# Re-ordering one Strassen product: w_out sum ahead, quadrant sums in halves, products over changing banks

## The chip, the cores and the metric

The kernel runs on one NeuronCore of a Trainium2 chip. The metric is the device time of one execution in microseconds (us). Five runs of the kernel before gave 303.01, 303.22, 303.43, 304.36 and 303.58 us; the median is 303.43 us.

The core has engines that each work through an instruction list of their own, in order: PE (matrix products, with PEld loading the stationary operand), DVE (vector), ACT (scalar, exp), POOL (vector work, and issuing DMAs of the software queue) and SP (issuing DMAs of the hardware queue, among them DMA transposes). They wait for each other by semaphores.

## What is computed

Sparse attention followed by a two-layer network with a leaky activation. There are 8 batches, 8 heads, 576 positions, head size 64.

```python
scores = scale * np.matmul(q, k.transpose(0, 1, 3, 2))
# heads 0-3: a local band of 32; heads 4-7: keys with the same position mod 32, not later
scores = np.where(masks[None], scores, -1e9)
attn = softmax(scores)                       # (8, 8, 576, 576)
x = np.matmul(attn, v).transpose(0, 2, 1, 3).reshape(4608, 512)
h = x @ w_in                                 # (4608, 2048)
g = np.maximum(h, 0.0) + alpha * np.minimum(h, 0.0)
out = g @ w_out                              # (4608, 512)
```

## The kernel before, in words

**Chunks.** The 4608 tokens are worked in nine chunks of 512. A chunk's first layer ("lin1") makes the activation gT (2048 features on 16 blocks of 128 partitions, 512 tokens); its second layer ("lin2") multiplies gT with w_out. Chunk 0 is done plainly by `lin2_piece`. Chunks 1 to 8 use a Strassen-like product (`lin2_sums`): gT and w_out are cut into two by two quadrants, and seven products of quarter size, of which four use sums of quadrants of gT (gsum g1 to g4, made per chunk by `g_sum`, line 711) and some use sums of quadrants of w_out (wsum w1, w2, w4 and w3, the last made in place in w_out; made once by `w_sums`, line 699), give the four output quadrants o11, o12, o21, o22. g2 = g1 - quadrant, g4 = quadrant - g2, so g1, g2, g4 follow from one another; g3 needs gT alone. Also w1, w2, w4 follow from one another.

**Banks.** The seven products accumulate in three PSUM banks called A, B and C (tiles `hb`, which lin1 uses too). Product 0, 2, 4 and 6 go to A, one on top of the other; 1 and 3 go to B; 5 goes to C. After each product its bank's state is read out: products 0, 1, 2 and 6 are copied by ACT (line 771: o11, o22, o12, o21), products 3, 4 and 5 are added by DVE into a copy made before (line 774: o12, o22, o11) and the result is stored by SP. The next product on the same bank has to wait for that read-out. Each product is two halves of eight matmuls (128x128 by 256 columns), index `i` = 0 to 13, two for each product. For chunk 1 the order of the products is 0, 5, 1, 2, 3, 4, 6.

**Attention between.** Attention of the batches to come is cut into pieces (scores with exp on ACT and a mask on POOL; PV products; transposes of q and k; transposes of the result), which are put between the matmul groups of lin1 and lin2, so that PE always has work. How many go after each group is an accumulated count, `acc += left / divisor`; in the second half of chunk 1 (i >= 16 in the outer loop, line 977) the divisor is 21.7. Scores, PV results and transposes use the rotating PSUM pool `ps` with three buffers (`tp`, `tt`, `pv`, `sph`, `xp`), and `sp` with one. A PV result is read by DVE: reciprocal (line 478) and multiplication (line 480) into x, or x16s for the strided pairs.

**Where the attention result goes.** It must become xT, with features on partitions. From batch 2 on three of four head pairs are turned by DMA transposes issued by SP: the two local pairs straight into xT (line 506), the first strided pair from x16s into `xs` (line 504), which ACT then copies into xT in `x_copy` (line 511). The fourth pair is turned by PE in `x_piece` (tile `xp`, line 490) and copied into xT by ACT (line 191). Chunk 2's lin1 (line 629) needs all four pairs of batch 2: its matmuls go over kk = 0 to 3, one for each pair, so kk = 2 needs the copy of `xs` and kk = 3 the copy of `xp`. ACT has these in its list in the order: exp of a score, copy of `xs`, exp of the other half of the score, copy of o21 (line 771), copy of `xp`.

**Loads.** POOL issues loads of v (`vl`, `stv`), of q and k (`qsd`, `ksd`) and of their last rows (`tl`); SP issues `ql`, `kl`, the stores and the transposes. `load_v(3, False)` and `load_v(3, True)` stand in the chunk loop at fixed places of chunk 1 (lines 971 and 975).

**Order written out by hand.** Chunk 0's lin2 is a list of tokens (lines 939 to 952): ("M", i) is a quarter of a lin2 group, "S", "K", "P", "X", "T", "t" are attention pieces, "I" calls a function, here among others `w_sums`, which DVE carries out. w1 and w2 are made near the start of this list, w4 is made near its end, w3 at the start of chunk 1 (line 963).

Of the kernel before, what the change touches and what calls it, by code (L numbers as in the profile page):

```python
# [31 lines left out]
def kernel(  # L32
# [10 lines left out]
    nc = tc.nc  # L43
    keep = tc.keep_in_program_order

    B, H, S, D = q.shape
# [487 lines left out]
    for g in range(7, npair + 2):  # L534
        c = g // 4
        a, p, t = g, g - 1, g + 1
# [28 lines left out]
        for i, (kind, fn) in enumerate(seq):  # L565
            extra = []
            if todo and i in nslots:
                left = len([z for z in nslots if z >= i])
# [31 lines left out]
    def attn_until(b):  # L600

        return max(i for i, (g, _) in enumerate(pieces) if g == 4 * b + 3) + 1

    def attn_step(end):
        run_masks()
        if pos["i"] < end:
            pieces[pos["i"]][1]()
            pos["i"] += 1
        while late:
            late.pop(0)()  # L610
        if defer:
            defer.pop(0)()
# [26 lines left out]
    def lin1_piece(n, m):  # L639
        if n not in gTs:  # L640
            gTs[n] = gpool.tile([128, 16, 512], F16, tag="gT", name="gT")
        if n == 0 and m < 3:
            hps = lin1_mm(n, m, (0,), False, True)
        else:
            hps = lin1_mm(n, m, (3, 2, 0, 1) if n == 1 else range(4), True, True)

        neg = npool.tile([128, 512], F32, tag="neg", name="neg")
        keep(nc.scalar.activation(neg, hps, AF.Relu, scale=-1.0))  # L648

        def fin():  # L650
            keep(nc.vector.scalar_tensor_tensor(  # L651
                gTs[n][:, m, :], neg, oma[:, m : m + 1], hps, op0=ALU.mult, op1=ALU.add))
        late.append(fin)
# [25 lines left out]
    def quad(t, i, j):  # L679

        return t[:, 8 * j : 8 * j + 8, 256 * i : 256 * i + 256]

    def wq(i, j):

        return wout16[:, 8 * i : 8 * i + 8, 256 * j : 256 * j + 256]

    def w_sums(eng, which):

        w1, w2, w4 = wsum
        w3 = wq(0, 1)  # L690
        steps = {
            1: (w1, wq(0, 1), wq(0, 0), ALU.subtract),
            2: (w2, wq(1, 1), w1, ALU.subtract),
            3: (w3, wq(1, 1), wq(0, 1), ALU.subtract),
            4: (w4, wq(1, 0), w2, ALU.subtract),
        }
        for z in which:
            o, x, y, op = steps[z]
            keep(eng.tensor_tensor(o, x, y, op=op))

    def g_sum(eng, n, which, k0, k1):

        g = gTs[n]
        g1, g2, g4, g3 = gsum
        o, x, y, op = {
            1: (g1, quad(g, 1, 0), quad(g, 1, 1), ALU.add),
            2: (g2, g1, quad(g, 0, 0), ALU.subtract),
            3: (g3, quad(g, 0, 0), quad(g, 1, 0), ALU.subtract),
            4: (g4, quad(g, 0, 1), g2, ALU.subtract),
        }[which]  # L710
        keep(eng.tensor_tensor(o[:, k0:k1], x[:, k0:k1], y[:, k0:k1], op=op))  # L711
# [3 lines left out]
    def store(n, i, j, osb, mts=(0, 1)):  # L715

        r0 = 512 * n + 256 * i + 128 * mts[0]
        keep(nc.sync.dma_start(
            out[r0 : r0 + 128 * len(mts), 256 * j : 256 * j + 256].rearrange("(m p) c -> p m c", p=128),
            osb[:, mts[0] : mts[-1] + 1]))  # L720

    def quiet(n):

        return n >= NCH - 2

    def lin2_sums(n, i):

        g = gTs[n]
        last = n == NCH - 1
        p, mt = ((0, 5, 1, 2, 3, 4, 6) if n == 1 else range(7))[i // 2], i % 2  # L730
        if i == 0:
            tiles = [banks[z] for z in turn]
            lay.clear()
            for nm, t in zip("ABC", tiles):
                lay[nm] = [t[:, 0:256], t[:, 256:512]]
                lay[nm + "f"] = t
            turn[:] = [turn[1], turn[2], turn[0]]
            if last:
                lay["A"][1] = pspool.tile([128, 512], F32, tag="ps", name="opl")[:, 0:256]
            g_sum(nc.vector, n, 1, 4 if n == 1 else 6, 8)  # L740
            g_sum(nc.vector, n, 2, 0, 4)
            g_sum(nc.vector, n, 2, 4, 8)
        if i == (1 if quiet(n) else 2):
            g_sum(nc.vector, n, 4, 0, 8)
        if i == (2 if quiet(n) else 4):
            g_sum(nc.vector, n, 3, 0, 8)
        bank, lhs, rhs, first = (
            ("A", quad(g, 0, 0), wq(0, 0), True),
            ("B", gsum[0], wsum[0], True),
            ("A", gsum[1], wsum[1], False),  # L750
            ("B", gsum[2], wq(1, 1), False),
            ("A", gsum[3], wq(0, 1), False),
            ("C", quad(g, 0, 1), wq(1, 0), True),
            ("A", quad(g, 1, 1), wsum[2], False),
        )[p]
        dst = lay[bank][mt]
        own = mt == 0 or (last and bank == "A")
        for kf in range(8):
            keep(nc.tensor.matmul(  # L759
                dst, lhs[:, kf, 128 * mt : 128 * mt + 128], rhs[:, kf, :],  # L760
                start=(first and own and kf == 0), stop=(kf == 7), skip_group_check=True))

        def each(fn, o, *more):

            if last and bank == "A":
                fn(o[:, mt], lay["A"][mt], *[z[:, mt] for z in more])
            elif mt == 1:
                fn(o, lay[bank + "f"].rearrange("p (m c) -> p m c", m=2), *more)

        def act(o, x):  # L770
            keep(nc.scalar.copy(o, x))  # L771

        def add(o, x, y):
            keep(nc.vector.tensor_tensor(o, x, y, op=ALU.add))  # L774

        def new(nm):
            if mt == 0:
                held[nm] = opool.tile([128, 2, 256], F32, tag="osb", name=nm)
            return held[nm]

        if p == 0:
            each(act, new("o11"))
        elif p == 1:
            each(act, new("o22"))
        elif p == 2:
            each(act, new("o12"))
        elif p in (3, 4, 5):
            r, c = ((0, 1), (1, 1), (0, 0))[p - 3]
            o = held[f"o{r + 1}{c + 1}"]
            each(add, o, o)  # L790
            if mt:
                store(n, r, c, o)
        else:
            o21 = new("o21")
            if last and mt:
                keep(nc.vector.tensor_copy(o21[:, 1], lay["A"][1]))
            else:
                each(act, o21)
            if last:
                store(n, 1, 0, o21, (mt,))  # L800
            elif mt:
                store(n, 1, 0, o21)
# [113 lines left out]
    def attn_n(n, end):  # L916
        for _ in range(n):
            attn_step(end)
        if n == 0:
            attn_step(0)  # L920
# [7 lines left out]
    for z in (3, 4):  # L928
# [10 lines left out]
    run([  # L939
        ("M", 0), ("I", w_sums, nc.vector, (1,)), ("M", 4), ("I", w_sums, nc.vector, (2,)),  # L940
        ("I", load_qk, 2, False, "q"), ("M", 5), ("M", 1), ("M", 6), ("T", 3, "q"), ("M", 2),
        ("T", 3, "k"), ("t", 3), ("V", 1, 1, "dve"), ("C", 1, "q", 1, "dve"),
        ("C", 1, "q", 0, "pool"), ("V", 1, 0, "pool"), ("M", 7), ("C", 1, "k", 1, "pool"), ("M", 3),
        ("S", 6), ("T", 2, "q"), ("K", 6), ("M", 8), ("S", 7), ("t", 2),
        ("I", load_qk, 2, False, "k"), ("K", 7), ("M", 9), ("C", 1, "k", 0, "pool"), ("T", 2, "k"),
# [2 lines left out]
        ("I", load_d, 2), ("K", 4), ("M", 12), ("P", 6, 2), ("S", 5), ("O", 1, "pool", 1, 12),  # L948
        ("P", 4, 0), ("O", 1, "pool", 12, 24), ("X", 7), ("M", 13), ("I", cast_l, 2, "k", "act"),
        ("K", 5), ("P", 4, 1), ("I", load_v, 2, True), ("X", 6), ("M", 14), ("P", 5, 0), ("G",),  # L950
        ("P", 5, 1), ("M", 15), ("X", 4), ("X", 5), ("I", w_sums, nc.vector, (4,)), ("G",),
    ])
    assert pos["i"] == 2
    wide["on"] = False
# [3 lines left out]
    for n in range(1, NCH):  # L958
        ab = attn_until(n + 1) if n + 1 < B else len(pieces)
        left = ab - pos["i"]  # L960
        acc = 0.0
        if n == 1:
            w_sums(nc.vector, (3,))
        for i in range(30):
            second["on"] = i >= 16
            if i < 16:
                lin1_piece(n, {13: 7, 14: 14}.get(i, 8 * (i % 2) + i // 2))
                if i in (5, 9, 13) and (n, i) != (1, 13):
                    g_sum(nc.gpsimd, n, 1, i // 2 - 2, i // 2)
                if n == 1 and i == 14:  # L970
                    load_v(3, False)
            else:
                lin2_sums(n, i - 16)
                if n == 1 and i == 22:
                    load_v(3, True)
            if n < B - 2 or i < 16 or i > 19:
                acc += left / ((22.5 if i < 16 else 21.7) if n == 1 else 16 if n == B - 2 else 20.5) * (0.5 if i < 16 else 1.0)
            cnt = int(acc)
            acc -= cnt
            attn_n(cnt, ab)  # L980
        while pos["i"] < ab:
            attn_step(ab)
# [30 lines left out]
```

## Time and profile before

The profile is of one execution, whose own time and span stand beside the runs.

| what | value |
|---|---|
| median of five runs | 303.43 us |
| time of the profiled execution | 303.01 us |
| its span, first to last instruction | 301.2 us |
| granted TensorE clock | 0.998 |
| busy share PE / DVE / ACT / POOL | 97 / 76 / 60 / 55 % |
| chunk 1's lin2 on PE, first matmul of product 0 to the first of chunk 2's lin1 | 73.63 to 91.68 us |
| wholes of g4 and g3 in chunk 1 (DVE) | 2.18 and 1.21 us |
| w4 (DVE), at 57.52 us | 1.22 us |
| xs transpose of batch 2, issue | 84.07 us |

The profile has several views. The page gives busy time for each engine. The stages view gives the busy time of each engine in stretches of the span that one chooses. The timeline lists instructions in order of time: start in us, duration in us, engine, line, operation, output <- inputs, shapes, how many of them; in square brackets, how long the engine stood idle just before and what released it. The chain of waits follows the work that ended last back to the start. The DMA view gives for each issue the time from issue to landing. A matmul's recorded duration is a modelled end and longer than the distance to the next one; the starts are measured.

### The profile page before, as it was taken

What the parts mean: (1) busy time and instruction counts of PE and PEld (TensorE: products, weight loads), DVE (VectorE), ACT (ScalarE), POOL (GpSimd) and SP (SyncE); (2) the same over time, 40 slices, a digit from 0 to 9 for tenths busy, and PEclk for the clock granted to TensorE, in tenths of its full rate; (3) what the DMA queues carried; (4) which work ended last, traced back from release to release, by engine and by line L of the source; (5) the groups of instructions that cost most, each with busy time, mean ns of one, the idle gap of its engine ahead of it and who ended that gap; (6) DMA issues with size and microseconds to landing.
All of it is one profiled execution on the core that took longest, in us unless ns stands there. A gap on an engine that the chain in (4) does not pass through costs nothing.

```text
span 301.2 us, 7137 instructions
## 1 busy us (share of the span) xinstructions
PE 291.9 (97%) x2823; PEld 195.9 (65%) x2823; DVE 227.9 (76%) x429; ACT 180.5 (60%) x334; POOL 167.0 (55%) x176
## 2 busy tenths in 40 slices
PE   8899999999898999999999999999999999999995
PEld 3564456645774478647888887458745874784584
DVE  5788959989955987498848884888488958946872
ACT  3757458789537773776477746775577246506720
POOL 8952369379939965976497639772746003101300
PEclk9999999999999999999999999999999999999999
DMA  7999999997999996999499729971921040022004
GB/s 221 197 204 207 205 236 249 171 159 257 145 152 182 241 115 51 172 260 126 66 201 240 99 43 182 139 99 27 194 55 20 9 154 2 0 71 72 0 2 139
DMA packets 81713, 40.38 MB, mean 134 GB/s; under 512 B 58624, under 2 KB 77328, under 8 KB 81680
## 3 DMA queue, kind: packets, MB, share of 16 engines
q0 software_dynamic: 41728, 17.38, 52.0%
q1 hardware_dynamic: 39680, 22.03, 33.6%
q10 hardware_dynamic: 272, 0.52, 0.6%
q8 instruction: 22, 0.36, 0.5%
q14 instruction: 11, 0.09, 0.1%
HBM read 38.01 MB, written 9.44 MB: 158 GB/s over the span
## 4 chain that ended last, share of the span: by engine, by line
PE 77%; DMA 12%; DVE 5%; POOL 3%; ACT 1%; issue 1%; POOLq 0%
PE hb L629 35%; PE hb L759 30%; DMA qs<-in_q_dram 6%; PE pv L469 4%; DMA vl<-in_v_dram 3%; DMA tl<-in_k_dram 3%; PE hb L666 2%; DVE gsum L711 2%; PE sp L421 2%; PE tp L255 2%; PE opl L759 1%; DVE gT L651 1%; PE sph L421 1%; PE xp L490 1%; POOL vl L195 1%
## 5 line engine op out<-in xcount | busy, mean ns | idle before, releaser
L629 PE MATMUL hb<-xT,win 128*128 128x512 f16 (+1 forms) x616 | 127.8, 357 | 1.1 <-ACT xT L191 0.9
L651 DVE SCALAR_TENSOR_TENSOR gT<-neg,oma,hb 128x512 f16<-128x512 f32 x138 | 100.6, 744 | 33.1 <-ACT neg L648 26.6
L648 ACT ACTIVATE neg<-hb 128x512 f32<-128x512 f32 x138 | 82.0, 597 | 34.8 <-PE hb L629 34.1
L629 PEld LDWEIGHTS <-win 128*128 128x128 f16 x640 | 59.8, 98 | 54.6 <-issue 1.3
L711 POOL TENSOR_TENSOR gsum<-gT 128x512 f16<-128x512 f16 x23 | 26.4, 1148 | 52.0 <-DVE gT L651 52.0
L436 POOL TENSOR_TENSOR et<-et,consts 128x576 f16<-128x576 f16 (+1 forms) x24 | 31.2, 1300 | 42.4 <-ACT et L434 36.5
L759 PEld LDWEIGHTS <-gsum 128*128 128x128 f16 x512 | 47.4, 98 | 5.6 <-DVE gsum L711 0.2
L759 PEld LDWEIGHTS <-gT 128*128 128x128 f16 x384 | 35.9, 98 | 5.8 <-issue 0.4
L480 DVE TENSOR_TENSOR x<-pv,rc 96x384 f16<-96x384 f32 (+2 forms) x62 | 33.0, 532 | 2.1
L771 ACT COPY o<-hb 128x512 f32<-128x512 f32 (+1 forms) x32 | 18.1, 567 | 25.9 <-PE hb L759 25.9
L443 POOL TENSOR_TENSOR et<-et,consts 128x576 f16<-128x576 f16 (+1 forms) x24 | 31.4, 1310 | 2.1 <-ACT et L440 2.1
L759 PE MATMUL hb<-wout,gT 128*128 128x256 f16 x248 | 31.3, 273 | 0.0
L759 PE MATMUL hb<-wout,gsum 128*128 128x256 f16 x248 | 31.0, 273 | 0.0
L469 PEld LDWEIGHTS <-et 72*128 72x128 f16 (+1 forms) x448 | 23.7, 98 | 10.0 <-DVE x16s L480 1.1
L759 PE MATMUL hb<-wsum,gsum 128*128 128x256 f16 x248 | 30.1, 272 | 0.0
L774 DVE TENSOR_TENSOR o<-hb,o 128x512 f32<-128x512 f32 (+1 forms) x24 | 16.3, 680 | 14.9 <-PE hb L759 11.0
L434 ACT ACTIVATE et<-sp 128x576 f16<-128x576 f32 (+1 forms) x24 | 15.5, 645 | 18.6 <-PE sp L421 18.6
L478 DVE RECIPROCAL rc<-pv 72x6 f32<-72x6 f32 (+2 forms) x80 | 14.6, 182 | 8.7 <-PE pv L469 8.5
L440 ACT ACTIVATE et<-sph 128x288 f16<-128x288 f32 (+1 forms) x48 | 18.9, 409 | 0.0
L469 PE MATMUL pv<-vs,et 72*128 72x65 f16 x256 | 15.4, 194 | 0.9 <-DVE x16s L480 0.8
L195 POOL COPY vs<-stv 72x1024 f16<-72x1024 f16 x14 | 14.2, 1033 | 3.2 <-DMA stv<-in_v_dram 3.2
L759 PE MATMUL hb<-wsum,gT 128*128 128x256 f16 x120 | 15.2, 273 | 0.4 <-DVE o L774 0.4
(109 smaller groups left out, 326.2 us busy)
## 6 DMA issues: line engine op xcount, KB each, us to landing
out_dram<-o SPq DMA_DIRECT2D x31, 256.0 KB, 4.2
kl<-in_k_dram SPq DMA_DIRECT2D x6, 512.0 KB, 6.4
ql<-in_q_dram SPq DMA_DIRECT2D x5, 512.0 KB, 6.0
stv<-in_v_dram POOLq DMA_DIRECT2D x8, 288.0 KB, 7.6
vl<-in_v_dram POOLq DMA_DIRECT2D x6, 384.0 KB, 9.8
win<-in_moe_w_in_dram POOLq DMA_DIRECT2D x4, 512.0 KB, 11.2
wout<-in_moe_w_out_dram POOLq DMA_DIRECT2D x4, 512.0 KB, 15.9
qsd<-in_q_dram POOLq DMA_DIRECT2D x6, 288.0 KB, 7.0
```

What stands on the lines that cost most here:

```text
L195: keep(nc.gpsimd.tensor_copy(o, i))
L436: keep(nc.gpsimd.tensor_tensor(mv, mv, m, op=ALU.mult))
L440: keep(nc.scalar.activation(ev[:, n * y : n * y + n], sps[y][0:r, 0:n], AF.Exp, scale=SCALE))
L443: keep(nc.gpsimd.tensor_tensor(mv, mv, m, op=ALU.mult))
L469: keep(nc.tensor.matmul(pv[:, 65 * x : 65 * x + 65], et[0:r, c : c + 128], v16[0:r, 2 * P.pr + hh, t, :] if P.strided else v16[:, 6 * (2 * ...
L480: keep(nc.vector.tensor_tensor(P.x16[0:w, c0 : c0 + 64 * nb].rearrange("r (c e) -> r c e", e=64), pvv[:, :, 0:64], rc[0:w, 0:nb].unsqueeze ...
L629: keep(nc.tensor.matmul(hps[:, dst : dst + w], win16[:, kk, 128 * m : 128 * m + 128], xT[:, kk, src : src + w], start=(first and kk == kks ...
L648: keep(nc.scalar.activation(neg, hps, AF.Relu, scale=-1.0))
L651: keep(nc.vector.scalar_tensor_tensor(gTs[n][:, m, :], neg, oma[:, m : m + 1], hps, op0=ALU.mult, op1=ALU.add))
L711: keep(eng.tensor_tensor(o[:, k0:k1], x[:, k0:k1], y[:, k0:k1], op=op))
L759: keep(nc.tensor.matmul(dst, lhs[:, kf, 128 * mt : 128 * mt + 128], rhs[:, kf, :], start=(first and own and kf == 0), stop=(kf == 7), skip ...
L771: keep(nc.scalar.copy(o, x))
```

## The change

Four things are changed, all of them for chunk 1 alone. (1) The w4 sum moves from the end of chunk 0's token list to its beginning, behind w2. (2) g3 and g4 of chunk 1 are each made in two halves of four blocks, g3 at i = 4 and 5, g4 at i = 6 and 7; before, g4 was made whole at i = 2 and g3 whole at i = 4. (3) The products' order becomes 0, 5, 2, 1, 4, 3, 6, so that the banks go A C A B A B A where before they went A C B A B A A. (4) In the second half of chunk 1 the divisor becomes 19.7, so that attention pieces come more densely and end earlier, and `load_v(3, True)` is called two steps earlier.

```diff
-        p, mt = ((0, 5, 1, 2, 3, 4, 6) if n == 1 else range(7))[i // 2], i % 2
+        p, mt = ((0, 5, 2, 1, 4, 3, 6) if n == 1 else range(7))[i // 2], i % 2
...
-        if i == (1 if quiet(n) else 2):
+        if n == 1:
+            if 4 <= i < 8:
+                g_sum(nc.vector, n, 3 if i < 6 else 4, 4 * (i % 2), 4 * (i % 2) + 4)
+        elif i == (1 if quiet(n) else 2):
             g_sum(nc.vector, n, 4, 0, 8)
-        if i == (2 if quiet(n) else 4):
+        elif i == (2 if quiet(n) else 4):
             g_sum(nc.vector, n, 3, 0, 8)
...
         ("I", load_qk, 2, False, "q"), ("M", 5), ("M", 1), ("M", 6), ("T", 3, "q"), ("M", 2),
-        ("T", 3, "k"), ("t", 3), ("V", 1, 1, "dve"), ("C", 1, "q", 1, "dve"),
+        ("I", w_sums, nc.vector, (4,)), ("T", 3, "k"), ("t", 3), ("V", 1, 1, "dve"), ("C", 1, "q", 1, "dve"),
...
-        ("P", 5, 1), ("M", 15), ("X", 4), ("X", 5), ("I", w_sums, nc.vector, (4,)), ("G",),
+        ("P", 5, 1), ("M", 15), ("X", 4), ("X", 5), ("G",),
...
-                if n == 1 and i == 22:
+                if n == 1 and i == 20:
                     load_v(3, True)
...
-                acc += left / ((22.5 if i < 16 else 21.7) if n == 1 else 16 if n == B - 2 else 20.5) * (0.5 if i < 16 else 1.0)
+                acc += left / ((22.5 if i < 16 else 19.7) if n == 1 else 16 if n == B - 2 else 20.5) * (0.5 if i < 16 else 1.0)
```

What this does to the instruction lists of the engines: on PE the pieces of attention from the second product on stand one half product earlier, and the list is the same again from chunk 2's first matmul on. On DVE the read-outs of the first two PV results into x16s come before the sums g3 and g4. On ACT the copy of `xp` comes before the copy of o21. On POOL the load of `stv` comes before the two `tl` loads instead of behind them.

## The prediction

> **What bounds the kernel now.** I read the page first: PE is busy 97% of the span at a granted clock of 0.998, so time can be won only where PE stands still. The chain of waits runs on PE nearly all the way, except from 69.5 to 83 us, where it passes through ACT and DVE. So I cut the span into stages and looked where PE is not busy.
>
> ```profile
> 62.00:73.60 11.60, 11.60 (x99) 5.65 (x98) 9.62 (x17) 9.89 (x20) 10.70 (x10) 1.00 0.93 183
> 73.60:91.70 18.10, 16.53 (x224) 13.96 (x220) 14.05 (x28) 9.77 (x18) 13.29 (x13) 1.00 1.47 177
> 91.70:93.40 1.70, 0.82 (x9) 0.30 (x6) 0.00 (x0) 1.61 (x4) 1.68 (x3) 1.00 0.36 66
> ```
>
> The columns are stage, length, then PE, PEld, DVE, ACT and POOL busy. Stage two is chunk 1's Strassen product, the one that is edited; stage three is the start of chunk 2. PE is full before them. The timeline names each stop (idle time and releaser in brackets):
>
> ```profile
> 60.71 1.46 PE L629 MATMUL hb<-xT,win 128*128 128x512 f16 x6 [0.20 <-DVE gT L651]
> ...
> 77.72 2.18 DVE L711 TENSOR_TENSOR gsum<-gT,gsum 128x2048 f16<-128x2048 f16 x1
> 78.79 2.24 POOL L443 TENSOR_TENSOR et<-et,consts 72x576 f16<-72x576 f16 x1
> 80.66 0.62 PE L255 MATMUL tp<-consts,kl 128*128 128x128 f16 x8 [0.34 <-DVE x16s L480]
> 81.11 1.21 DVE L711 TENSOR_TENSOR gsum<-gT 128x2048 f16<-128x2048 f16 x1
> 83.08 0.30 PE L469 MATMUL pv<-vs,et 72*128 72x65 f16 x4 [0.81 <-DVE x16s L480]
> 84.07 1.21 SPq L504 DMA_TRANSPOSE xs<-x16s  x1
> 89.49 1.03 PE L759 MATMUL hb<-wsum,gT 128*128 128x256 f16 x8 [0.42 <-DVE o L774]
> 90.68 1.31 ACT L511 COPY xT<-xs 128x576 f16<-128x576 f16 x1 [0.69 <-DMA xs<-x16s]
> 91.90 0.40 ACT L440 ACTIVATE et<-sph 128x288 f16<-128x288 f32 x1
> 92.20 0.57 ACT L771 COPY o<-hb 128x512 f32<-128x512 f32 x1
> 92.67 0.65 ACT L191 COPY xT<-xp 128x576 f16<-128x576 f16 x1
> 93.37 0.81 PE L629 MATMUL hb<-xT,win 128*128 128x512 f16 x3 [0.88 <-ACT xT L191]
> ```
>
> Five stops, 2.65 us as shown. They cost more: eight 256-column matmuls pass in 0.87 us in the chain of waits, 0.109 each, while one is recorded as 0.272, so each stop hides 0.16 more. From start to start the stops lose 0.26 + 0.50 + 0.98 + 0.48 + 1.04 = 3.26 us (the first and fourth without the 0.10 that every score block costs on each side here). After 93.4 us the timeline shows PE starts without any such gap to the end, so what is won up to there should be kept.
>
> **Part 1, w4 moved.** Before, w4 takes DVE for 1.22 us at 57.52. ACT's tail copy of kT waits 0.35 for the tail copy of qT queued behind it, so the first `neg` starts at 59.06 and the first gT ends at 60.67, when PE needs it at 60.45. Without w4 ACT goes on at 58.55, `neg` ends about 59.33, gT about 60.08: the stop goes, **-0.26**. Next late is nothing: the second gT comes 0.75 later, PE asks 0.87 later. In its new place w4 follows w2 (ends 38.29) and DVE is idle for 2.30 us up to 40.60, so 1.22 fits: 0. POOL issues loads there; its two issues under w1 and w2 took 0.64 and 0.62, as alone (0.63), so again 0. At worst the vl load issued at 38.82 starts 0.7 later, and nobody needs it before 51.6.
>
> **Part 2, quadrant sums in halves and later.** Three PSUM tiles rotate through scores, transposes and PV. At 80.66 a transpose waits for DVE to read out a PV, queued behind g4 (2.18); at 83.08 a PV waits for the next read-out, queued behind g3 (1.21). In the new instruction order both read-outs come before the sums: x16s one ends near 78.25, two near 79.65, when PE asks for the tiles at 78.9 and 80.3. Both stops go, **-1.48**. Four halves at 0.68 (the row of the g2 halves) instead of two wholes at 1.21 are 0.30 us more of DVE, which then idles. By my walk g3 is whole near 81.5 and needed at 82.9, g4 near 83.4 and needed at 84.9; each slack is 1.4.
>
> [...]
>
> **Part 3, product order A C A B A B A.** The last product no longer meets bank A just after the product whose sum DVE still reads; that add (0.69) lies under the two B products, **-0.48**. The second A product, now right after C, needs g2 (ends about 77.4, asked for at 78.0) and bank A copied out (ACT, 76.19 to 76.78): 0. The next A product needs its o12 copied, near 81.5 against 82.9: 0.
>
> **Part 4, denser attention.** No instruction is added; from the second product on attention pieces move one half product (0.87) ahead. The first PV is then asked for at 75.57, while the tile it reuses is read out until 75.62 plus signalling: **+0.10**. Its masks are done (72.8 and 74.0). POOL is the serial engine here (10.70 of 11.60 us busy) and no mask moves ahead of its exp; with stv issued two steps earlier POOL's order becomes stv, tl, tl, and stv goes out near 80.1 instead of 82.28, with no one queued behind it but the tails, needed a chunk later. On ACT the xT copy of the last pair passes the o21 copy: 92.67 - 92.20 = 0.47 off the way to chunk 2. PE reaches chunk 2 at 91.68 - 0.26 - 1.96 + 0.10 = 89.56 and wants its fourth matmul (kk = 3) at 90.21.
>
> **Part 5, what is late next.** That matmul ran at 93.37. ACT was busy without a break from 90.68, when xs landed: copy, exp, o21, xT. With o21 out, kk = 3 can run at landing + 2.24 (93.37 - 0.47 - 90.66). Only a landing before 88.0 would give all of it. xs is issued when the third read-out ends: 82.1 against 84.07. When does it land? The DMA view, for the stretch 76 to 91 and for chunk 2:
>
> ```profile
> xs<-x16s SPq DMA_TRANSPOSE x1, 6.6
> ...
> xs<-x16s SPq DMA_TRANSPOSE x1, 4.4
> ```
>
> If it takes 6.6 again, it lands at 88.7, kk = 3 runs at 90.94 and the gain is 2.43. [...] The software queue holds vl, qsd, ksd, tl and stv from 74 on, and its last, stv, lands at 82.28 + 8.0 = 90.3; xs landed 0.4 after that, and the same transpose took 4.4 in chunk 2, where the software queue had nothing in that stretch. [...] The new xs has more of the crowded stretch ahead of it, but can use turns that its own queue may leave free between 82 and 85, when only one store and the end of one transpose stand before it; I take the middle, 89.7: kk = 3 at 91.92, **gain 93.37 - 91.92 = 1.45**.
>
> **Sum.** The profiled execution took 303.01 (span 301.2 and 1.8 around it); 303.01 - 1.45 = 301.56. Its time is the lowest of five, 0.42 under the median of 303.43, so the median becomes 301.98, predicted 302.0. The four stops inside (2.22) are won, and about 1.7 us comes back as a longer stop at the head of chunk 2.
>
> **The rivals.**
> - The drain rules (30%): xs lands at 90.3 to 90.7, gain 0.3 to 0.9, median about 302.9. For it: xs landed just behind stv. Against it: the stretch 82 to 85 has room in xs's own queue.
> - The transfer follows its issue or better (22%): landing 86.5 (82.1 + 4.4) to 88.7; gain 2.4 to 3.16, median near 300.6. For it: 4.4 in chunk 2. Against it: six loads are in flight.
> - Slower (6%): xs is overtaken. The o11 store (256 KB) goes out near 79 instead of 81.22 and stv 2 us sooner, both into the stretch in which pair 9's xT transpose took 10.0 us; if they push xs behind qT and kT's traffic, ACT, in order, holds xT, o21 and the first `neg` behind it. It decides from a landing after 91.1 (90.66 + 0.47) and passes the measurable from 92.0; at 93.3, where qT landed (85.38 + 7.9), the median would be 305.6. Against it: that same traffic was all ahead of xs before too.
> - My forecast (42%): landing 88.8 to 90.2, gain 0.9 to 2.3.
>
> That the change does not do what it says is out: the new order on each engine shows it.
>
> **Numbers.** A measurement of this kernel can tell about 0.3% (0.9 us) from no change. Faster by more: the forecast and the early landing, 0.64. Within: the drain, 0.30. Slower: 0.06. The range runs from nearly all stops won (303.43 - 3.16 = 300.3) to the drain with its smallest gain, 303.2.
>
> **What would show it.** Right: no PE idle on x16s between 76 and 83 nor on the o add before the last product; PE at chunk 2's first matmul near 89.5; xs issued near 82, landed near 89.7, ACT idle before the xs copy, and PE waiting about 1.7 us in two pieces (for the xs copy, then for xT). The drain: the same with landing beyond 90.2. Wrong: new idle on g3 or g4, a PV that waits for a POOL mask, w4 delaying the gT of chunk 0 or a first-pass read-out, or new gaps after chunk 2 has begun.

## The result and the profile after

The changed kernel takes 303.11 us (median of 43 runs, 300.71 to 309.74) against 303.64 for the kernel before (80 runs in the same comparison): a ratio of 0.9975, with a 95% interval of 0.9961 to 0.9989, or by that ratio 0.76 us less (0.53 between the medians). The ratio leaves out runs more than 1.5% above the fastest of their kernel. I had predicted 302.0, a gain of 1.45. The sign is right; the size is about half.

The profiled execution took 301.8 us, 1.2 less than the one of before, and it does nearly what the prediction said. The stages first (stage, length, then PE, PEld, DVE, ACT and POOL busy, the granted clock, DMA share, GB/s):

```profile
62.00:74.00 12.00, 12.00 (x99) 5.82 (x98) 9.84 (x18) 10.29 (x22) 11.85 (x11) 1.00 0.70 171
74.00:90.32 16.32, 16.30 (x223) 13.98 (x221) 13.17 (x30) 8.93 (x18) 12.55 (x12) 1.00 1.39 187
90.32:92.17 1.85, 0.98 (x6) 0.29 (x4) 0.00 (x0) 1.85 (x4) 1.83 (x3) 1.00 1.47 90
```

The product now lasts 16.3 us and PE is busy in all of it; before, the same work took 18.1 with 16.5 busy. What is left is the third row, the head of chunk 2. The timeline, at the places where before stood still:

```profile
61.13 1.90 PE L629 MATMUL hb<-xT,win 128*128 128x512 f16 x8
...
79.90 0.61 PE L255 MATMUL tp<-consts,kl 128*128 128x128 f16 x8
...
81.33 0.29 PE L469 MATMUL pv<-vs,et 72*128 72x65 f16 x4
...
82.38 1.25 SPq L504 DMA_TRANSPOSE xs<-x16s  x1
...
88.31 1.04 PE L762 MATMUL hb<-wsum,gT 128*128 128x256 f16 x8
...
89.97 1.31 ACT L511 COPY xT<-xs 128x576 f16<-128x576 f16 x1 [1.74 <-DMA xs<-x16s]
91.33 0.38 PE L629 MATMUL hb<-xT,win 128*128 128x512 f16 x1 [0.42 <-ACT xT L511]
91.49 0.63 ACT L191 COPY xT<-xp 128x576 f16<-128x576 f16 x1
92.17 2.10 PE L629 MATMUL hb<-xT,win 128*128 128x512 f16 x9 [0.46 <-ACT xT L191]
```

Four PE rows that carried a bracket before have none. ACT, which stood idle for 0.69 us before the copy of xs, now does so for 1.74, and PE waits at two places, for that copy and for the copy of xT behind it. From start to start these two stops lose 0.58 and 0.62 us. The DMA view has the landing of xs, 7.6 us after its issue where before had 6.6:

```profile
xs<-x16s SPq DMA_TRANSPOSE x1, 7.6
```

From chunk 1's first matmul to the fourth of chunk 2 this execution needs 34.08 us (58.09 to 92.17) where before needed 35.97 (57.40 to 93.37): 1.89 less. But chunk 1 began 0.69 later, and 1.89 - 0.69 = 1.20 is the difference of the two executions. The 0.69 comes from chunk 0, which the prediction had put at 0. The first two rows are of before, in the timeline:

```profile
50.30 2.29 POOL L195 COPY vl<-vl 32x715 f16<-32x715 f16 x2
51.08 0.81 DVE L329 TENSOR_TENSOR et<-et,consts 128x576 f16<-128x576 f16 x2
```

and these of after:

```profile
50.48 1.78 POOL L195 COPY vl<-vl 32x715 f16<-32x715 f16 x2
50.87 1.71 DVE L329 TENSOR_TENSOR et<-et,consts 128x576 f16<-128x576 f16 x2
51.63 0.36 PE L469 MATMUL pv<-vl,et 128*128 128x65 f16 x6 [0.25 <-DVE et L329]
53.18 0.36 PE L469 MATMUL pv<-vl,et 128*128 128x65 f16 x6
53.87 0.43 PE L490 MATMUL xp<-consts,x 72*128 72x72 f16 x8 [0.33 <-DVE x L480]
```

The same two POOL copies and the same two DVE masks meet, and now the masks take longer and the copies less: before, the copies take 2.29 and the masks 0.81; after, 1.78 and 1.71. PE, which was 0.21 us ahead of before until then, pays for the second order with stops of 0.42, 0.24 and 0.50 us, where before lost 0.16 and 0.10.

A last thing is seen in the times and not in this execution. Each run has a mean granted clock. Of the 44 runs of the changed kernel (the profiled one too) 29 have 0.998 or more, with a median of 302.27. The other 15 have 0.986 to 0.994 and take 303.8 to 309.7, with a median of 306.15. Without those, the gain would be 303.64 - 302.27 = 1.37, nearly the forecast (the clocks of the 80 runs of before are not listed in this comparison). This is what the experiments pursue.

### The profile page after: what moved, and what is told of

It is laid out like the page before. It is cut to its first block, busy times and chain, and to the rows that moved or that the text cites. A ratio compares the mean times of both kernels' runs of the same rounds, so it can differ in the third digit from the quotient of the medians.

```text
span 300.0 us, 7141 instructions
## 1 busy us (share of the span) xinstructions
PE 291.5 (97%) x2823; PEld 195.4 (65%) x2823; DVE 228.2 (76%) x431; ACT 180.1 (60%) x334; POOL 166.4 (55%) x176
## 3 DMA queue, kind: packets, MB, share of 16 engines
q1 hardware_dynamic: 39680, 22.03, 32.7%
## 4 chain that ended last, share of the span: by engine, by line
PE 77%; DMA 14%; DVE 3%; POOL 3%; issue 1%; ACT 0%; ACTq 0%; DVEq 0%; POOLq 0%
PE hb L629 37%; PE hb L762 29%; DMA qs<-in_q_dram 6%; PE pv L469 3%; DMA vl<-in_v_dram 3%; DMA xs<-x16s 3%; DMA tl<-in_k_dram 2%; PE tp L255 2%; PE sp L421 2%; PE opl L762 1%; PE hb L666 1%; DVE x L480 1%; PE sph L421 1%; PE xp L490 1%; DVE et L329 1%
## 5 line engine op out<-in xcount | busy, mean ns | idle before, releaser
L648 ACT ACTIVATE neg<-hb 128x512 f32<-128x512 f32 x138 | 82.1, 597 | 34.6 <-PE hb L629 33.9
L436 POOL TENSOR_TENSOR et<-et,consts 128x576 f16<-128x576 f16 (+1 forms) x24 | 31.9, 1328 | 42.4 <-ACT et L434 35.5
L711 POOL TENSOR_TENSOR gsum<-gT 128x512 f16<-128x512 f16 x23 | 26.4, 1148 | 52.0 <-DVE gT L651 52.0
L777 DVE TENSOR_TENSOR o<-hb,o 128x512 f32<-128x512 f32 (+1 forms) x24 | 16.3, 681 | 16.1 <-PE hb L762 12.4
L666 PE MATMUL hb<-wout,gT 128*128 128x512 f16 x64 | 15.6, 379 | 0.0
## 6 DMA issues: line engine op xcount, KB each, us to landing
wout<-in_moe_w_out_dram POOLq DMA_DIRECT2D x4, 512.0 KB, 16.3
```

The lines of the kernel that those rows point to most:

```text
L436: keep(nc.gpsimd.tensor_tensor(mv, mv, m, op=ALU.mult))
L666: keep(nc.tensor.matmul(ops, gTs[n][:, kf, 128 * mt : 128 * mt + 128], wout16[:, kf, :], start=(kf == 0), stop=(kf == 15)))
```

## The experiments

Four theories. **G**: PE's stops are now gathered at the head of chunk 2, and there the clock falls to half in some runs. **C**: xs lands when the transfers in flight have drained, however early it is issued (the prediction's rival). **W**: w4 in its new place brings the stops of chunk 0. **T**, formed later: xs lands late where the transpose of pair 9 meets the vl load. The recorded expectations use more letters: A is the first form of G (a lower clock in some runs), B is W; N (the stops of chunk 0 come and go, whatever is done to w4) and S (the early store and stv load, or the chip, delay xs) are rivals. "Low-clock runs" are those with a mean clock under 0.995; no run has a value between 0.994 and 0.997. Their share is given as "5 of 22".

### The parts, apart

**e1, the changed kernel again**, with no edit.

> The changed kernel again, beside the kernel before on the same chip. Theory A (granted clock): at a full granted clock of 1.00 the changed kernel is 1.4 us faster than before, and the measured 0.76 is what is left because some of its runs get a clock near 0.993, which costs 0.7% of some 290 us of PE, 2 us; so runs sorted by their clock fall into groups 2 us or more apart, and those at 1.00 lie near 302.2. Theory B (w4): every run is 0.7 us late at the start of chunk 1, as in the profiled one (chunk 1's first matmul at 58.09 instead of 57.40), so the gain is 0.7 at any clock. Theory C (landing): the time varies with the landing of xs; this profile shows a stop at the head of chunk 2 other than 1.2 us.

302.48 us (10 runs), ratio 0.996 [0.9938, 0.9983]; 1 of 10 low-clock (before on this chip 0 of 23). In its profile xs lands 8.0 us after its issue and the two stops at the head of chunk 2 are 1.04 and 0.62; the stops of chunk 0 are there again.

**e2, only w4 moved.**

```diff
+        ("I", w_sums, nc.vector, (4,)), ("T", 3, "k"), ("t", 3), ("V", 1, 1, "dve"), ("C", 1, "q", 1, "dve"),
...
-        ("P", 5, 1), ("M", 15), ("X", 4), ("X", 5), ("I", w_sums, nc.vector, (4,)), ("G",),
+        ("P", 5, 1), ("M", 15), ("X", 4), ("X", 5), ("G",),
```

> Only the w4 sum is moved; sums, product order and attention as before. Theory B: it is the loss: chunk 1 begins near 58.1 and the time is 0.4 to 0.7 us above before. Theory A, and the prediction: -0.26 at the head of chunk 1, which the later wait for xs takes back, so between 0 and -0.26, not measurable; chunk 1 begins near 57.4, give or take what the run to run difference of the first stage is.

303.59 us, ratio 1.0001 [0.9986, 1.0016], no low-clock run in 13. The gT stop at the head of chunk 1 is gone (from the first matmul of chunk 1 to the product 15.97 us instead of 16.23, as predicted), and the stops of chunk 0 have come (0.41, 0.23, 0.50). As a whole it gains nothing.

**e3, all but w4**: the edit of e2 undone in the changed kernel.

> The changed kernel with w4 made where it was before. Theory B: faster than the whole change by 0.4 to 0.7 us, so 1.2 to 1.5 us below before. Theory A: like the whole change within 0.3 us, since w4 gives only 0.26 which the wait for xs takes back. Theory C: the same as A.

302.14 us, ratio 0.9954 [0.9942, 0.9967], 1 of 6 low-clock. No stops of 0.4 to 0.5 in chunk 0; the product takes 16.26 us; stops of 0.80 and 0.62 at the head of chunk 2. So the three other parts give all of the gain that can be measured; of these only the sums were tried by themselves (e7).

**e7, only the sums in halves and later.** In the old order of products g4 is asked for first, so it is made first here.

```diff
+        if n == 1:
+            if 4 <= i < 8:
+                g_sum(nc.vector, n, 4 if i < 6 else 3, 4 * (i % 2), 4 * (i % 2) + 4)
```

> Only the quadrant sums in halves and later, on the kernel before; the fourth before the third, since the old order of products asks for it first. By the prediction's steps both stops inside (0.50 and 0.98) go and xs is issued near 82.4 instead of 84.07. If the landing binds (theory C), it lands near 90, the xT copy of the last pair still waits for o21, and the fourth matmul of chunk 2 runs at landing + 2.7 = 92.6: a gain of 0.7, near 302.8, with the stop of 0.48 before the last product kept and simply filled into the wait. If the parts add up (rival), the gain is 1.48, near 302.0.

302.36 us (22 runs), ratio 0.9982 [0.996, 1.0004], 5 of 22 low-clock; the other 17 have a median of 302.11. Both inner stops are gone, the one before the last product stays (0.48 as the prediction counts it). xs, issued at 83.50, lands at 90.82, and kk = 3 runs at 93.53, which is landing + 2.71, as theory C has it, for o21 is still ahead of the xT copy. From chunk 1's first matmul that is 35.20 us, 0.77 less than before. The two do not agree: the trace has C's gain, near 0.7, but the 17 runs lie 1.48 under before, which is just what the rival said. One profile is one landing.

### Does an earlier issue bring an earlier landing?

The profiles of the kernels that keep pair 10's DMA transpose answer it. Counted from the first matmul of chunk 1 (issue, landing): before 26.7, 33.3; e2 26.4, 31.2; e12 (below) 26.4, 31.0; e7 25.2, 32.5; e3 24.6, 32.3; the changed kernel 24.3, 31.9; e1 24.3, 32.3; e16 (below) 24.3, 32.7. The three that issue xs latest have it at 31.0 to 33.3, the four that issue it earliest at 31.9 to 32.7: issued two microseconds sooner, xs does not land sooner. The DMA view of e2, where xs was issued latest:

```profile
xs<-x16s SPq DMA_TRANSPOSE x1, 4.8
```

4.8 us there, 7.6 in the changed kernel. These landings agree with theory C. I had taken the middle between this and a landing that follows the issue; that it came near (89.95 for 89.7) is in part luck, for the reason I gave, room left in xs's own queue, is not what these profiles show.

One thing holds in all fifteen profiles with this transpose: xs lands within 0.7 us of the last of the loads that POOL issues at that time (stv and the two tl), whether these end at 88.7 us (e13, xs at 88.9) or at 93.7 (e9, below, xs at 93.6). For the changed kernel, and for e5 (below):

```profile
tl<-in_k_dram POOLq DMA_DIRECT2D x1, 32.0 KB, 8.2
...
tl<-in_k_dram POOLq DMA_DIRECT2D x1, 32.0 KB, 12.4
```

Issued at 81.81 and 80.78 us, they land at 90.0 and 93.2; xs lands at 90.0 and 92.9. In the five profiles without the transpose these loads end at 89.3 to 93.4, so they can end late without it.

### Is it the stop that costs the clock?

**e8, the stop made longer**: ACT copies the transposed pair 10 twice.

```diff
-        keep(nc.scalar.copy(
...
+        for _ in range(2 if P.g == 10 else 1):
+            keep(nc.scalar.copy(
```

> The changed kernel, with ACT's copy of the transposed pair 10 done twice over, so that PE's stop at the head of chunk 2 is 1.3 us longer (2.5 to 3.0 in all within some 4 us). Theory G (a concentrated stop lets PE's clock fall to half for one 3.4 us unit, in some runs): the runs with a mean clock under 0.995 become the rule, and the median is 1.3 + 1.7 to 2.0 over that of the changed kernel, near 305.5; the profile shows a piece of half clock after 92. Rival (the low clock in some runs has nothing to do with this stop): nearly all runs stay at 0.998 or more and the median is 303.7.

305.49 us (17 runs), ratio 1.0049 [1.0026, 1.0073]. The six runs at full clock have 303.71, as both theories had it; 11 of 17 are low-clock, ten of them at 0.992 to 0.994 with a median of 305.95. In the profile the two stops are 1.88 and 0.62 us, and the stages (the column before the last two is the clock) show what follows:

```profile
91.60:93.90 2.30, 0.61 (x4) 0.21 (x3) 0.00 (x0) 2.27 (x3) 2.28 (x3) 1.00 1.23 119
...
95.20:98.60 3.40, 3.40 (x15) 1.33 (x14) 1.49 (x2) 1.21 (x4) 3.40 (x4) 0.52 1.08 281
98.60:102.00 3.40, 3.40 (x35) 1.57 (x32) 2.71 (x5) 2.66 (x6) 0.69 (x2) 1.00 1.24 326
```

For one stretch of 3.4 us the clock is about half: 0.52, with 0.94 in the 1.3 us ahead of it and 1.00 behind. The nine matmuls from the end of the second stop on take 3.76 us, where the same nine took 2.10 in the changed kernel's profile (its row at 92.17): 1.7 us lost. (The counts of matmuls in the two stretches, 15 and 35, mix long and short ones.) In this run the half clock came after stops of 1.88 and 0.62; why some runs have it and others do not is not shown. Theory G holds as far as this: with the longer stop more runs lose their clock, 11 of 17 for 20 of 68.

**e5, w4 left out.** It is not computed at all, and the last product takes w2.

```diff
-            ("A", quad(g, 1, 1), wsum[2], False),
+            ("A", quad(g, 1, 1), wsum[1], False),
...
-        ("I", w_sums, nc.vector, (4,)), ("T", 3, "k"), ("t", 3), ("V", 1, 1, "dve"), ("C", 1, "q", 1, "dve"),
+        ("T", 3, "k"), ("t", 3), ("V", 1, 1, "dve"), ("C", 1, "q", 1, "dve"),
```

> The changed kernel without the w4 sum: it is not computed at all, and the last product takes w2 in its place, so its output is not the reference's. Theory W (w4 in its new place turns the order in which DVE masks and POOL copies get their turn in chunk 0, and that costs the stops of 0.4, 0.2 and 0.5 us there): the stops at 51 to 56 us are absent, the gT stop at the head of chunk 1 is absent too, and the median is 1.6 us under before, near 301.8. Rival N (those stops come and go with the landing of kl, whatever is done to w4): they can be there, chunk 1 begins as late as in the changed kernel, and the median is that of the changed kernel, near 302.4.

303.87 us (22 runs), ratio 0.9986 [0.9967, 1.0006]; 7 of 22 low-clock (before on this chip 2 of 58), the other 15 with a median of 302.50. The profile happened on a low-clock run (0.988) and shows one such run. Its DMA view, timeline and stages:

```profile
xs<-x16s SPq DMA_TRANSPOSE x1, 11.5
```

```profile
89.29 0.59 PE L629 MATMUL hb<-xT,win 128*128 128x512 f16 x2
92.89 1.31 ACT L511 COPY xT<-xs 128x576 f16<-128x576 f16 x1 [5.69 <-DMA xs<-x16s]
94.25 0.58 PE L629 MATMUL hb<-xT,win 128*128 128x512 f16 x1 [4.36 <-ACT xT L511]
```

```profile
89.29:92.80 3.51, 0.59 (x4) 0.19 (x2) 0.00 (x0) 0.00 (x0) 1.87 (x2) 1.00 1.56 78
92.80:96.20 3.40, 1.70 (x4) 0.51 (x4) 0.00 (x0) 3.13 (x5) 3.38 (x5) 0.51 1.11 197
96.20:99.60 3.40, 3.40 (x14) 1.39 (x13) 1.49 (x2) 1.12 (x3) 3.40 (x4) 0.50 1.07 238
```

xs lands 11.5 us after its issue instead of 7.6. PE, which reached chunk 2 at 89.29, over a microsecond sooner than in the changed kernel's profile, stands still for 4.5 us and then has half clock for 6.8 us, in some 5 of which it works. So in this run the late landing comes first, and the clock is the second payment for it.

**e9, PE kept busy in the stop**: seven matmuls of a zero tile, added into the same bank.

```diff
+            if n == 2 and m == 0 and kk >= 2:
+                for _ in range({2: 4, 3: 3}[kk]):
+                    keep(nc.tensor.matmul(
+                        hps, zer, win16[:, 0, 0:512], start=False, stop=False, skip_group_check=True))
```

> The changed kernel with seven 512-column matmuls of a zero tile at the head of chunk 2 (four before the fourth-last wait, for pair 10's xT, three before the wait for pair 11's), added into the same PSUM bank, so that PE works through 1.5 us of the 1.2 to 1.7 us in which it would stand still; the waits themselves stay. Theory G (the clock falls to half in some runs because PE stands still there): no run, or hardly any, under a mean clock of 0.995, where the changed kernel had 15 of 44; the median is that of its undisturbed runs plus at most 0.3, near 302.4. Rival (low-clock runs have another cause, for instance the chip): the low-clock runs stay about a third.

303.25 us (22 runs), ratio 0.9978 [0.9956, 1.0], and still 7 of 22 low-clock: the expectation failed. The profile, again of a low-clock run (0.987), shows a reason: xs landed 12.1 us after its issue, and PE stood still for 4.26 us behind the first six matmuls (two of chunk 2, four of zeros). 1.5 us of work cannot cover that.

**e4, pair 10 turned by PE** in the changed kernel, so that nothing at the head of chunk 2 waits for a DMA transpose.

```diff
-        P.xd = P.b >= DX and P.hp < 3
+        P.xd = P.b >= DX and P.hp < 3 and g != 10
```

> The changed kernel, with the first strided pair of batch 2 turned by PE (8 more matmuls of 72 columns, about 0.25 us) and not by a DMA transpose, so that chunk 2 no longer waits for a landing. All theories: the two stops at the head of chunk 2 (0.58 and 0.62 in the profile after) go, and with the 0.25 us for the matmuls the time is 0.9 us below the whole change. Theory C, that the landing mostly comes later than in the profiled run: more than 1.2 us below it, and less spread from run to run. If the next thing that is late (the copy of the last pair on ACT) takes their place: no more than 0.3 us.

302.21 us (5 runs), ratio 0.9961 [0.9948, 0.9974], none low-clock. The stop at the head of chunk 2 is gone. In the profile a new one has come (0.90 and 0.25 near 81): the additional piece shifts the attention, and two halves of g2 that meet two POOL masks (1.29 and 1.74) take 3.47 us instead of 1.28. The median is only 0.27 under e1's on the same chip, the case in which something else takes the stop's place.

**e6, the same with w4 in its old place**, and with the attention of chunk 1's first half kept where it was (one piece taken off the count `left` while i < 16).

> All of the change but the w4 move, and pair 10 turned by PE instead of by the DMA transpose; the attention of the first half of chunk 1 keeps its places. Theory: the wait at the head of chunk 2 is for the transposed pair alone, and the four stops inside were really won. Then PE stops only for the gT (0.36) and the first PV (0.2) and does 8 transposes more (0.26): 3.26 - 0.36 - 0.10 - 0.26 = 2.5 us under before, near 300.9, with every run at a mean clock of 0.998 or more, since PE nowhere waits longer than 0.4. Rival: DVE's second g2 half meets a POOL mask again as with pair 10 on PE before (3.47 for two halves, 0.90 + 0.25 of stop): near 302.0.

301.88 us (10 runs), ratio 0.9944 [0.9925, 0.9964], none low-clock. The new stop is gone, the product takes 16.25 us, and at the head PE waits only for pair 11's copy, 0.47 from start to start. The profiled execution took 301.17, near the forecast of 300.9; the median missed it by 1 us. The rows:

```profile
90.38 0.81 PE L629 MATMUL hb<-xT,win 128*128 128x512 f16 x3
91.49 2.10 PE L629 MATMUL hb<-xT,win 128*128 128x512 f16 x9 [0.30 <-ACT xT L191]
```

With its repetition e11 and with e4, e10 and e17 there are 44 runs with pair 10 on PE, and none is low-clock. Of the changed kernel's it is 20 of 68 (e1 and e16 included). This ties the low-clock runs to the wait for the transpose of pair 10. The kernel before has that transpose too, but reaches it later; in the batches whose clocks are listed it has 7 of 197.

### Is it w4's place?

**e10**, e6 with w4 moved as in the change; **e11**, e6 again, beside it on the same chip; **e12**, e2 again.

> The whole change, w4 move included, with pair 10 turned by PE and the attention of the first half of chunk 1 in its places: it differs from the kernel beside it in this batch by w4's place alone. By the prediction's step (the move gains 0.26 at the head of chunk 1 and costs nothing): 0.26 under that kernel. Theory W (w4 in its new place brings the stops of chunk 0, 0.4 + 0.24 + 0.5 against 0.15): 0.4 to 0.6 over it, and the profile shows those stops. Rival N (chance): equal or under it, and no such stops in one of the two profiles with w4 moved.

> The same kernel as e6 again, as the one to set the kernel before it against, on the same chip: 301.9, stops at 51 to 56 of no more than 0.2 by theory W; by rival N they can be 0.4, 0.24 and 0.5 here too.

> Only the w4 move, on the kernel before, again: by theory W the stops of chunk 0 are there in the profile and the median is 0.1 to 0.6 over the kernel before; by the prediction's step 0.26 under it, and by rival N the stops may be missing.

e10 301.73 us (11 runs), ratio 0.9936 [0.9916, 0.9956]; e11 302.13 (6 runs), 0.9933 [0.9908, 0.9959]; e12 303.50 (14 runs, 1 low-clock), 0.9986 [0.9968, 1.0004]. The medians of e10 and e11 differ by 0.40 for w4's new place, as the prediction's 0.26 would have it, but the ratios do not tell them apart. All three profiles have the stops of chunk 0, e11 too, where w4 is in its old place, and so has e7; e6, the same kernel as e11, has none. Theory W as a rule falls. Over all profiles the stops are there in 12 of 14 with w4 moved and in 2 of 6 with it in its old place or left out: whether the move makes them likelier stays open.

### Why does xs land late in some runs?

In e5 and e9 the transpose of pair 9 was issued 1.6 and 1.7 us behind the vl load, and vl took 10.7 and 10.9 us; in the changed kernel it was 2.6 us and 7.4. That was theory T.

**e13, the vl load issued three steps of the first half earlier** (`i == 11` for `i == 14`); **e14, later** (at `i == 18`, behind two masks, `qsd` and `ksd`); **e15, pair 9 turned by PE** (`g != 9`, with the count of e6); **e16, the changed kernel again** on the same chip.

> The changed kernel with POOL's issue of the vl load moved ahead of the two masks of pair 9's successor, 2.5 us earlier; nothing else. Theory T (xs lands late, 11.5 to 12 us after its issue, where pair 9's transpose is issued less than 1.8 us behind the vl load and the two drag each other): the distance becomes 4 us and more, vl lands within 7 us of its issue, no run has a mean clock under 0.995, and the median is that of the changed kernel's undisturbed runs or better, 301.8 to 302.3. Rival S (the early stv load and store, or the chip, delay xs): a fifth to a third of the runs stay at a lower clock, as in the changed kernel beside it.

> The changed kernel with the vl load issued behind the masks and qsd and ksd, just ahead of stv (about 78.9): now pair 9's transpose is ahead of it and xs has all of vl and stv ahead of it in the other queue. [...] Rival (only the meeting of vl with pair 9's transpose is dear): xs lands by 90, no low-clock runs, near 302.

> The changed kernel with pair 9 turned by PE, so that no transpose runs beside the vl load; pair 10's transpose stays with the DMA. Theory T: vl lands within 7 us, xs lands 4.5 to 6 us after its issue (82.7), about 88, no low-clock runs; PE does 6 transposes more (0.26) and stops at the head of chunk 2 for 0.5 or less: near 301.3. Rival S: low-clock runs stay; xs lands at 90 or later as before.

> The changed kernel again, beside those: 302.3 in the undisturbed runs; under theory T the low-clock runs (a tenth to a third) are there on this chip too, near 305; it sets their share for the three others.

| | median us (runs) | ratio | low-clock | xs, issue to landing | stops at the head |
|---|---|---|---|---|---|
| e13 | 302.22 (8) | 0.9944 [0.992, 0.9969] | 1 of 8 | 6.3 | none |
| e14 | 303.98 (22) | 1.0013 [0.9991, 1.0035] | 5 of 22 | 10.2 | 1.33, 0.62 |
| e15 | 302.11 (22) | 0.996 [0.9943, 0.9977] | 2 of 22 | 4.6 | 0.72 |
| e16 | 302.95 (14) | 0.9983 [0.9958, 1.0009] | 4 of 14 | 8.4 | 1.39, 0.62 |

e13 looked like T, though vl took 9.4 us and not the 7 that T asked for. For e14 I had estimated by C that xs lands 3 us or more behind the changed kernel's 89.95, that pair 9's transpose takes 4 to 6 us instead of 9.6, and that the median is over 305 with most runs at a lower clock. The landing was late, though less late (91.6 and not 93), with a median 1 us under 305 and most runs at full clock; pair 9's transpose took 7.5 us, not 4 to 6; and PE waits 1.87 us for vl itself before the last product, which I had not expected. e15 fits T in the 4.6 us of its transpose, but not in its median, expected near 301.3, nor in its 2 low-clock runs, where T had none.

**e17, e10 with the vl load earlier; e18, e13 again.**

> The whole change with pair 10 turned by PE and the vl load issued ahead of the masks, 2.5 us earlier: nothing at the head of chunk 2 waits for a transpose by the DMA. By theory: no run under a mean clock of 0.995, the stops of the product and the head (but 0.2 and 0.47) gone, and the median 1.7 to 2.2 us under the kernel before, 301.5 to 302.0, as e10. Rival (vl earlier costs something elsewhere): over 302.2.

> The same kernel as e13 again, for the share of low-clock runs: theory T gives none or one of ten, and near 302.1 for the rest; rival S gives a fifth to a third, as in the changed kernel (20 of 68 over three batches).

e17 301.59 us (12 runs), ratio 0.9931 [0.9903, 0.996], none low-clock on a chip where before has 4 of 23: the lowest median of all, and clearly better than the kernel before. On this chip, with vl at the same place, e17 has 0 of 12 and e18, which keeps the transpose, 4 of 12. e18 303.74 us (12 runs), ratio 0.9987 [0.9954, 1.0021]. Its DMA view:

```profile
vl<-in_v_dram POOLq DMA_DIRECT2D x1, 384.0 KB, 11.2
```

Pair 9's transpose was issued 5.1 us behind vl, and vl took 11.2 us all the same; xs took 8.6. With e13 that is 5 of 20 low-clock, which cannot be told from the changed kernel's 20 of 68. Theory T falls as the cause. xs lands with the end of POOL's loads; what makes these end late in some runs stays open. One regularity is in the profiles: e5, e9 and e14 are those whose chunk 1 began earliest (57.05, 57.15, 56.81; their chunk 0 was without the stops), and in them xs landed latest, 34.8 to 36.4 us after that, against 30.2 to 33.3 in the twelve others. An earlier PE did not bring an earlier landing there. Whether the one causes the other was not tried; nor was the earlier store and the earlier stv load apart from the rest.

## Why the prediction was half right

**Stops inside the product.** Predicted -1.48 (sums) and -0.48 (order), +0.10 for the first PV. With the transposes of the last pair counted on both sides the product took 18.05 before and takes 16.26: -1.79, for a sum of -1.86. Right, and in e7 the sums alone take away their two stops. The first PV's new stop is 0.19 from start to start.

**w4.** -0.26 at the head of chunk 1: 16.23 to 15.97 us, exact. "0" in its new place: w4 fits into DVE's gap there (38.3 to 39.5 us), as said; whether it has a part in the later stops of chunk 0 is open. But e2 and e12 as a whole gain nothing that can be measured.

**Head of chunk 2.** Forecast landing 89.7 and kk = 3 at 91.92; the profiled execution has 89.95 and 92.17, landing + 2.22 for the 2.24 of the sum. Here the trace is within 0.25 us of the forecast. PE, though, came there at 90.32 instead of 89.56, for chunk 1 began 0.69 late, and so stood still for 1.20 us and not for about 1.7. That the landing was right all the same is in part luck; it fits theory C, in which it does not follow PE.

**Terms of that sum that no run shows.** That room in xs's own queue brings its landing forward from 90.66, which gave the middle of 89.7, is shown by no run; the runs show a landing within 0.7 us of the last load that POOL had issued, whether that ended at 88.7 us (e13) or at 93.7 (e9). Its 82.1 for the end of the third x16s read-out was my estimate of how the sums and the masks would meet; in the profiled execution that read-out ends at 82.35 (81.93 + 0.42) and xs is issued at 82.38. The halves of g3 take 0.68 us each there and the two of g4 1.28, and the mask that meets the halves of g2 takes 2.56, where the next one takes 1.27.

**The step that failed** is the last term of the sum: "about 1.7 us comes back as a longer stop at the head of chunk 2", with the landing as one number, "I take the middle, 89.7". In e5 and e9 the landing came at 92.87 and 93.56, 11.5 and 12.1 us after the issue, where the range of my cases for it ended at 90.7 except for the rival "xs is overtaken" (6%), which had 305.6 us for a landing at 93.3. Such runs are not rare: 20 of 68 of the changed kernel have the low clock that goes with them, and their times (median 306.15 in the first comparison) are near that rival's, in part by luck, for it priced no loss of clock. They put the median from 302.27 to 303.11: 0.84 of the 0.92 us between forecast and gain per median (1.45 and 303.64 - 303.11 = 0.53). No profile of the changed kernel shows a low-clock run (its three have landings of 7.6 to 8.4 us); that its low-clock runs are like those of e5 and e9 is inferred from the 44 runs of the kernels without that transpose, in which there is none.

**The second half of the same term.** I priced the stop at its length. In e8 stops of 1.88 and 0.62 us cost a stretch of half clock besides, 1.7 us; in e5 the clock was half for 6.8 us. Before, 3.26 us of standing still lay in five places of at most 1.04, and low-clock runs were 7 of 197. The change made PE arrive sooner at a landing that did not come sooner, and so turned four short stops into a longer one.

## What to carry to other kernels

When stops on the critical engine are won ahead of a wait for a transfer, ask first whether that transfer lands sooner, what it lands together with, and over which range it lands from run to run: one trace gives one landing. Stops gathered into one place can cost more than their sum (in e8 a stretch of 3.4 us at a clock of 0.52 followed stops of 1.88 and 0.62, and cost 1.7 us besides); so the wait itself should be taken away (here eight transposes on PE, 0.26 us) before the stops ahead of it are. And where short instructions of two engines meet, which of them takes longer can turn over (two masks took 0.81 us before and 1.71 in the changed kernel), and the stops of PE behind it can be absent in one run and present in the next of the same kernel (e6, e11); what it costs is seen only over several profiles.

## What the runs showed of the hardware

- The same program's transpose of 80x1024 took 6.3 us from issue to landing in one profile and 8.6 in the next (e13, e18), and 4.6 to 12.1 over all kernels. In all fifteen profiles it landed within 0.7 us of the last load that POOL had issued at that time.
- A clock near half came in stretches of 3.4 us (e8, 0.52) and 6.8 us (e5, 0.51 and 0.50); stops of 1.58 and 0.62 (e18, mean clock 1.00) passed without it in the one execution profiled, 1.88 and 0.62 (e8, mean clock 0.993) did not.
- Two POOL copies and two DVE masks cost 2.29 and 0.81 us or 1.78 and 1.71 us, in the two orders in which they met; PE stood still there for 0.26 us with the first (before) and 1.16 with the second (the changed kernel).
